# Second softmax by way of DRAM, PSUM banks of a batch end dealt out anew, last rows with W_out itself

## Chip, cores and metric

One core of a Trainium2 chip. The time is that of one execution on the device, in microseconds; lower is better.

## What is computed

x is [8, 8, 512, 64] (batch, head, token, dim), state [8, 8, 32, 64]. Per batch and head both attend to each other, and the 544 rows of a batch, heads side by side, go through one wide layer:

```python
a  = softmax(scale * x @ state.T)      # 512 x 32, scale = 1/8
xread = a @ state                      # token rows
a2 = softmax(scale * state @ x.T)      # 32 x 512, the second softmax
sread = a2 @ x                         # state rows
X = concat([xread, sread], axis=2)     # [8 * 544, 512] after heads are laid side by side
h = X @ w_in                           # 512 -> 2048
g = where(h >= 1, h, where(h <= -1, 0, (h + 1)**2 / 4))
out = g @ w_out                        # 2048 -> 512
```

All is float32. A product is made of three fast ones: both factors are split into a high and a low part, and high x high, low x high and high x low are summed.

## The kernel before

The work runs over batches b = 0 to 7 of 512 token rows, then b = 8, the 256 state rows of all batches together. Each batch has 8 steps (b, j), of 256 hidden columns each. Batch 0 is put in order by a planner with costs (`Plan`); from batch 1 on the order is that of the program: `direct` for batch 1, `sevenfold` for batches 2 to 8. Each engine runs its own instructions in program order, and a tile's buffer is handed on when its last reader is done.

A step of `sevenfold` has on TensorE: the first product (`Seven.product(0)`, 6 matmuls of 512 columns), half of the outer product of the step before (`outer(0)`), the second product, `outer(1)`. The outer product is done by seven block products instead of eight, over sums of g and of W_out's quarters; 42 matmuls of 256 columns. Their seven results stay in PSUM for the whole batch: 1 and 2 in the double buffer "mm", 7 in one of two "h" buffers, 4, 6, 5 and 3 in the four "acc" buffers, in this order (L745 to L749). `Gather` reads them out at the first step of the next batch, with three kinds of work: copies on ScalarE (`keep`, L784), additions on VectorE (`add`, L792), and four accumulating DMAs on POOL (`join`, L801); SP then writes the rows out (L806).

The sums of W_out's quarters are made in batch 1 (`fold_whole` to `fold_low`) and kept in DRAM in the tensors "fold", [128, 2, 7, 256] per chunk of 256 hidden columns; `load_wide` (L659) brings two tiles wd of 896 KB for each step, called two steps ahead, on SP.

The batch end, `stretch`, comes after the first step of a batch. TensorE reads the states of this batch (`read2`, sr, L401), multiplies the states into w_in for seven chunks and the next batch's first (`sw_product`, L449, four of them), and makes the next batch's scores (`att_start`, sc, L233), which ScalarE parks in SBUF (`park_all`, L243). Each state product is split by a cast (`sw_high`) and a subtraction (`sw_low`). sr and the "h" buffers, the first state product and the scores in "mm", the others in "acc" follow one another.

The second softmax: scores are on partitions by head pair and state; after exp, `turn_blocks` or `blocks_all` transposes 32 x 32 blocks into eb, and `shuffle` (L389) sends the blocks to the partitions of their tokens with 16 DMAs from SBUF to SBUF in runs of 128 bytes (32 KB each): batches 0 to 2 on SP, the others on POOL. For batch 0 the target is srT's buffer. `place2` (L419) sends the state rows of a batch into srT with 16 DMAs of 4 KB on POOL. SP's order in batch 1 is: shuffle of batch 0 in step 4, copies into "fold" (L636, L637), shuffle of batch 2 in step 5, "fold" again, tokens xn of batch 2 (L190) and the first wd.

The last rows (b = 8) take the same path as the others in 8 steps with 128 columns instead of 256, each w_in chunk split by `wi_split`; at the end `gather_states` makes the rows by one copy and nine additions and writes them in 16 DMAs of 32 KB.

Of the kernel before, what the change touches and what calls it, by code (L numbers as in the profile page):

```python
# [100 lines left out]
def state_exchange_moe(  # L101
# [73 lines left out]
    wo = {}  # L175

# [27 lines left out]
    class Attention:  # L204
# [10 lines left out]
        def scores(self, half=None):  # L215
            b = self.b
            if half != 1:
                sc = ps_mm(f"sc{b}")
                self.sc = [[sc[:, hh]] for hh in range(2)]
                self.z = work.tile([P, 2, S], F32, tag="z", bufs=1, name=f"z{b}")  # L220
                self.m1 = small.tile([P, 2 * NM], F32, tag="m1", name=f"m1_{b}")
                self.s1 = small.tile([P, 2 * NM], F32, tag="s1", name=f"s1_{b}")
            else:
                for hh in range(2):
                    self.sc[hh].append(ps_h(f"sc{b}_{hh}"))
            for pr in range(NPR):
                for hh in range(2):
                    rows = slice(hh * 64, hh * 64 + 64)
                    o = self.sc[hh][-1][pr * NS:(pr + 1) * NS]
                    m = self.xt[rows, :, pr]  # L230
                    if half is not None:
                        o, m = o[:, :S // 2], m[:, half]
                    nc.tensor.matmul(o, lhsT=sb[rows, b, pr], rhs=m, start=True, stop=True)  # L233
# [66 lines left out]
        def blocks_all(self):  # L300
            self.blocks = work.tile([P, 2, S], F32, tag="tmp", name=f"eb{self.b}")
            nc.vector.transpose(
                out=self.blocks.rearrange("p q t -> p (q t)"), in_=self.e2.rearrange("p q t -> p (q t)")
            )
# [69 lines left out]
        def turn_blocks(self, q):  # L374
            if q == 0:
                self.blocks = work.tile([P, 2, S], F32, tag="tmp", name=f"eb{self.b}")
            nc.vector.transpose(out=self.blocks[:, q], in_=self.e2[:, q])

        def shuffle(self):
            b = self.b  # L380
            self.r2 = small.tile([P, 2], F32, tag=own("r2", b), name=f"r2_{b}")
            nc.vector.tensor_scalar_add(self.r2, self.sum2, 1e-9)
            nc.vector.reciprocal(out=self.r2, in_=self.r2)
            src, dst = (
                v.rearrange("p q (t r n) -> p (q t) r n", r=NPR, n=NS) for v in (self.blocks, self.e2)
            )
            for r in range(NPR):
                for pr in range(NPR):
                    (nc.gpsimd if b > 2 else nc.sync).dma_start(  # L389
                        out=dst[r * NS:(r + 1) * NS, :, pr], in_=src[pr * NS:(pr + 1) * NS, :, r]  # L390
                    )

        def read2(self):
            b = self.b
            xn = loaded.pop(("xn", b))
            self.sr = ps_h(f"sr{b}")[:, :2 * D].rearrange("p (q d) -> p q d", q=2) if b else ps_mm(f"sr{b}")[:, :, :D]
            for q in range(2):
                for t in range(NT):
                    for pr in range(NPR):
                        rows = slice(pr * NS, (pr + 1) * NS)  # L400
                        nc.tensor.matmul(  # L401
                            self.sr[rows, q], lhsT=self.e2[:, q, t * P + pr * NS:t * P + (pr + 1) * NS],
                            rhs=xn[t][:, 2 * pr + q], start=t == 0 and (not b or q == 0), stop=t == NT - 1 and (not b or q == 1),
                        )
# [10 lines left out]
        def place2(self):  # L415
            b = self.b
            for k in range(P // NS):
                for pr in range(NPR):
                    nc.gpsimd.dma_start(  # L419
                        out=srT[k * NS:(k + 1) * NS, pr, b], in_=self.rt[pr * NS:(pr + 1) * NS, k * NS:(k + 1) * NS]  # L420
                    )


# [232 lines left out]
    def load_wide(b, c):  # L656
        pair = [wop.tile([P, 7, 256], F32R, tag="wo", name=f"wd{b}_{c}_{i}") for i in range(2)]
        for i in range(2):
            nc.sync.dma_start(out=pair[i].bitcast(F32), in_=folded[c][:, i])  # L659
        wide[b, c] = pair  # L660

    class Seven:
# [145 lines left out]
    def gather_states():  # L808

        o = rawp.tile([P, 2, DM], F32, tag="raw", name="o_states")  # L810
        e = work.tile([P, 3, 256], F32, tag="tmp", name="e_states")
        k = {m: v[:, :256] for m, v in banks[B].items()}

        def quad(t, d):
            return o[:, t, d * 256:(d + 1) * 256]

        def put(t, d):
            for i in range(4):
                r0 = (4 * t + i) * TOK + S
                (nc.sync if i % 2 else nc.scalar).dma_start(  # L820
                    out=out[r0:r0 + NS, d * 256:(d + 1) * 256], in_=quad(t, d)[i * NS:(i + 1) * NS]
                )

        def add(to, a, c, op=ALU.add):
            nc.vector.tensor_tensor(out=to, in0=a, in1=c, op=op)

        nc.scalar.copy(out=e[:, 0], in_=k[1])
        add(e[:, 1], k[7], e[:, 0])
        add(quad(0, 0), k[2], e[:, 0])
        put(0, 0)  # L830
        add(e[:, 2], k[4], e[:, 1])
        add(quad(1, 0), k[6], e[:, 2])
        put(1, 0)
        add(e[:, 0], k[6], e[:, 0])
        add(e[:, 1], k[6], e[:, 1])
        add(e[:, 0], k[5], e[:, 0])
        add(quad(1, 1), k[5], e[:, 1])
        put(1, 1)
        add(quad(0, 1), e[:, 0], k[3])
        put(0, 1)  # L840

    outs = {}

    def store(b, t):
        if b and t % 2 == 0:
# [131 lines left out]
    def att_start(b, half=None):  # L977
        if half != 1:
            atts[b] = Attention(b)
        atts[b].scores(half)  # L980
# [160 lines left out]
    steps = [(b, j) for b in range(1, B + 1) for j in range(NJ)]  # L1141
# [64 lines left out]
    for b in range(2, B):  # L1206
        attention(b)
    later("low", 1, 0, (fold_whole, 0))
# [24 lines left out]
    for i, s in enumerate(order[3:]):  # L1233
        later("last", *order[i + 1], (load_wide, *s))
# [4 lines left out]
    for c in range(2, NJ):  # L1239
        later("end", B, c - 2, (wi_split, c))  # L1240

    def rest(b, c):
        sw_high(b, c)
        sw_low(b, c)

    def stretch(b, between=None):
        final = b + 1 == B
# [5 lines left out]
        if not final:  # L1253
            att_start(b + 1)
        rest(b, 3)
        sw_product([(b, 7), (b + 1, 0)][:1 if final else 2], ps_acc, "raw")
        if between:
            between.high(1)
            between.low(1)
            between.last_sums()  # L1260
        atts[b].scale2()
        rest(b, 5)
        if not final and between:
            atts[b + 1].park_all()
        rest(b, 7)
# [21 lines left out]
    def sevenfold(b, j, prior, before):  # L1287
# [3 lines left out]
        first = j == 0 and b < B  # L1291
        now.product(0)
        now.curve(0)
        if old and old.b < B:
            old.high(2)
        now.bound(0)
        now.first_sum()
        if old and old.b < B:
            old.low(2)
        if b == B:  # L1300
            now.last_sums()
            for k in range(3):
                now.high(k)
                now.low(k)
            old.outer(0)
            if gather:
                gather.keep(1)
                gather.keep(7)
                gather.add(2)
            old.outer(1)  # L1310
            if gather:
                gather.add(6)
                gather.keep(4)
                gather.add(5)
                gather.keep(3)
                joins(gather, b)
            return now
# [27 lines left out]
        if first:  # L1345
            stretch(b, now)
# [5 lines left out]
        return now  # L1352

    with guard:
        plan.emit(warm)
        before = None
        for i, (b, j) in enumerate(steps):
            prior = steps[i - 1] if i else (0, NJ - 1)
            if b == 1:
                direct(b, j, prior)  # L1360
            else:
# [7 lines left out]
        before.outer(0)  # L1369
        before.outer(1)  # L1370
        gather_states()
# [43 lines left out]
```

## Time and profile before

| | us |
|---|---|
| three runs, median | 652.5 (652.27 to 653.89) |
| the profiled execution | 650.2 |
| its span | 648.4 |
| TensorE busy | 619.6 |
| VectorE busy | 517.8 |
| ScalarE busy | 475.4 |
| POOL busy | 158.4 |

Busy is the time in which an engine works on at least one instruction. PE is TensorE, PEld its weight loads, DVE VectorE, ACT ScalarE; SPq marks DMAs that SP issues. A DMA issue is not counted as busy time. Matmuls are pipelined: the length of one (283 or about 395 ns) is longer than the distance between the starts of two that follow one another.

### The profile page before, as it was taken

Reading aid. Unit: us, or ns where it says so; the run is one execution under the profiler, and the core shown is the slowest. Engines: PE = TensorE matmul, PEld = TensorE weight load, DVE = VectorE, ACT = ScalarE, POOL = GpSimd, SP = SyncE. Lnnn points to the kernel's source line nnn. Section 1 sums busy time; section 2 is a strip of 40 time slices with the busy share of each in tenths; the row PEclk is TensorE's granted clock in tenths of the full one; section 3 lists DMA queues with packets and bytes.
Section 4 is the critical chain, followed back from the end, with each engine's and each line's share of the span. In section 5 each row is a group of like instructions: output and inputs, shape, how many; then the busy total and the mean of one; then the engine's idle time right before and its main releaser. Section 6 shows DMA issues by size and latency. Waiting matters only on the chain.

```text
span 648.4 us, 13420 instructions
## 1 busy us (share of the span) xinstructions
PE 619.6 (96%) x5226; PEld 536.7 (83%) x5226; DVE 517.8 (80%) x824; ACT 475.4 (73%) x779; POOL 158.4 (24%) x260
## 2 busy tenths in 40 slices
PE   8999999998699999999999999999999999999994
PEld 3677787886579997999889997999799979999993
DVE  6999969895569977898689867987889777677773
ACT  6998766763567778787778777877877776777772
POOL 0000203111031501635162535250343206000100
PEclk9999999998999999999999999999999999999998
DMA  8993387877999887899879987999689986964985
GB/s 350 415 410 123 95 266 259 290 212 180 291 415 376 264 297 235 233 309 316 298 243 285 271 340 207 288 298 346 201 235 265 336 294 155 312 254 165 340 291 196
DMA packets 61967, 177.57 MB, mean 274 GB/s; under 512 B 22608, under 2 KB 31440, under 8 KB 58960
## 3 DMA queue, kind: packets, MB, share of 16 engines
q1 hardware_dynamic: 44576, 153.31, 67.9%
q0 software_dynamic: 16800, 23.08, 14.7%
q8 instruction: 41, 0.67, 0.4%
q10 hardware_dynamic: 528, 0.33, 0.2%
q14 instruction: 22, 0.18, 0.1%
HBM read 139.46 MB, written 26.21 MB: 256 GB/s over the span
## 4 chain that ended last, share of the span: by engine, by line
PE 76%; DVE 5%; DMA 3%; SPq 2%; ACT 2%; issue 2%; DVEq 0%; ACTq 0%
PE p L763 13%; PE p L762 13%; PE p L761 13%; PE h L692 8%; PE h L693 8%; PE h L694 8%; PE sw L449 4%; SPq L389 2%; PE acc L604 2%; PE acc L602 2%; PE acc L603 2%; DMA wd<-fold 2%; PE sr L401 1%; PE sc L233 1%; PE h L514 1%
## 5 line engine op out<-in xcount | busy, mean ns | idle before, releaser
L713 DVE SCALAR_TENSOR_TENSOR sums<-sums,over 128x512 f32<-128x512 f32 x104 | 71.7, 689 | 69.2 <-ACT sums L709 67.7
L762 PE MATMUL p<-wd,gh 128*128 128x256 f32 x416 | 117.9, 283 | 3.3 <-DMA wd<-fold 3.3
L763 PE MATMUL p<-wd,gl 128*128 128x256 f32 x416 | 117.7, 283 | 0.0
L761 PE MATMUL p<-wd,gh 128*128 128x256 f32 x416 | 117.3, 282 | 0.0
L734 ACT CAST gh<-sums 128x512 fp32r<-128x512 f32 (+1 forms) x112 | 65.6, 592 | 60.3 <-DVE sums L713 33.1
L707 ACT ACTIVATE sums<-h,half 128x512 f32<-128x512 f32 x104 | 71.8, 690 | 36.8 <-PE h L694 36.0
L763 PE MATMUL p<-wd,gc 128*128 128x256 f32 x312 | 88.8, 285 | 0.7 <-DVE gc L738 0.7
L761 PE MATMUL p<-wd,gc 128*128 128x256 f32 x312 | 88.3, 283 | 0.0
L762 PE MATMUL p<-wd,gc 128*128 128x256 f32 x312 | 88.3, 283 | 0.0
L762 PEld LDWEIGHTS p<-wd,gh 128*128 128x128 f32 x416 | 79.3, 191 | 7.4 <-DMA wd<-fold 3.7
L761 PEld LDWEIGHTS p<-wd,gh 128*128 128x128 f32 x416 | 79.3, 191 | 4.1
L763 PEld LDWEIGHTS p<-wd,gl 128*128 128x128 f32 x416 | 79.3, 191 | 0.0
L419 POOL DMA_DIRECT2D srT<-rt x128 | 63.2, 509 | 65.2 <-DVE rt L413 31.6
L738 DVE TENSOR_TENSOR gl<-sums,gh 128x512 fp32r<-128x512 f32 (+1 forms) x112 | 71.8, 647 | 0.7 <-ACT gh L734 0.7
L708 ACT ACTIVATE over<-h,less_one 128x512 f32<-128x512 f32 x104 | 70.9, 682 | 0.0
L709 ACT ACTIVATE sums<-sums 128x512 f32<-128x512 f32 x104 | 65.6, 631 | 0.0
L389 POOL DMA_DIRECT2D e<-eb x80 | 46.5, 587 | 72.2 <-ACT sums L709 51.5
L763 PEld LDWEIGHTS p<-wd,gc 128*128 128x128 f32 x312 | 59.8, 192 | 1.2 <-DVE gc L738 0.9
L761 PEld LDWEIGHTS p<-wd,gc 128*128 128x128 f32 x312 | 59.8, 192 | 0.0
L762 PEld LDWEIGHTS p<-wd,gc 128*128 128x128 f32 x312 | 59.8, 192 | 0.0
L604 PE MATMUL acc<-wo,gl 128*128 128x512 f32 x128 | 50.5, 395 | 0.5 <-DVE gl L564 0.5
L602 PE MATMUL acc<-wo,gh 128*128 128x512 f32 x128 | 50.7, 396 | 0.0
(260 smaller groups left out, 1473.8 us busy)
## 6 DMA issues: line engine op xcount, KB each, us to landing
wd<-fold SPq DMA_DIRECT2D x112, 896.0 KB, 7.8
xt<-in_xt_dram SPq DMA_DIRECT2D x16, 512.0 KB, 5.1
raw_i<-in_moe_w_in_dram SPq DMA_DIRECT2D x8, 1024.0 KB, 9.6
raw_o<-in_moe_w_out_dram SPq DMA_DIRECT2D x8, 1024.0 KB, 12.2
out_dram<-o SPq DMA_DIRECT2D x32, 256.0 KB, 4.8
fold<-wa POOLq DMA_DIRECT2D x8, 1024.0 KB, 5.9
xn<-in_x_dram SPq DMA_DIRECT2D x7, 1024.0 KB, 6.7
fold<-wo SPq DMA_DIRECT2D x8, 512.0 KB, 7.0
```

The source lines that it names most:

```text
L419: nc.gpsimd.dma_start(out=srT[k * NS:(k + 1) * NS, pr, b], in_=self.rt[pr * NS:(pr + 1) * NS, k * NS:(k + 1) * NS])
L602: nc.tensor.matmul(a, lhsT=lh, rhs=oh, start=f == 0, stop=False)
L604: nc.tensor.matmul(a, lhsT=ll, rhs=oh, start=False, stop=f == NF - 1)
L707: nc.scalar.activation(out=g, in_=h, func=AF.Relu, scale=0.5, bias=half)
L708: nc.scalar.activation(out=r, in_=h, func=AF.Relu, scale=1.0, bias=less_one)
L709: nc.scalar.activation(out=g, in_=g, func=AF.Square)
L713: nc.vector.scalar_tensor_tensor(out=g, in0=g, scalar=1.0, in1=r, op0=ALU.min, op1=ALU.add)
L734: nc.scalar.copy(out=gh, in_=s)
L738: nc.vector.tensor_tensor(out=gl, in0=s, in1=gh.bitcast(F32), op=ALU.subtract)
L761: nc.tensor.matmul(o, lhsT=gh[:, sl], rhs=wh, start=opens, stop=False)
L762: nc.tensor.matmul(o, lhsT=gh[:, sl], rhs=wl, start=False, stop=False)
L763: nc.tensor.matmul(o, lhsT=gl[:, sl], rhs=wh, start=False, stop=closes)
```

## The change

Four parts. `shuffle` writes the transposed blocks to a DRAM tensor "moved" in one DMA and reads them back in four, in runs of 1 KB; the transposition before it lays the blocks so that this works, and `read2` takes its columns accordingly. `place2` writes the rows of a batch to DRAM ("rows2") in one DMA, and `place_all` reads all batches' into srT in 16 DMAs on SP in step (7,2). At the batch end from batch 2 on, `stretch_between` takes the place of `stretch`: sr and the scores lie in "acc", the first state product in "h", the second in "mm"; state product 7 is split in step 1 of the batch ("curved"), and the third cast and subtraction (`high(2)`, `low(2)`) of step 0 come before it; banks 6 and 4 change places. `rest` casts and subtracts bank by bank. The last rows go in 4 steps (`last_rows`) of two chunks each, with plain products against W_out (`g2`), of which the missing quarter is now kept in "fold" as an eighth part, and are stored straight from two banks.

```diff
+    rows2 = drams.tile([B, P, P], F32, tag="rows2", bufs=1, name="rows2")
...
-            nc.vector.transpose(out=self.blocks[:, q], in_=self.e2[:, q])
+            nc.vector.transpose(out=self.by_rank(self.blocks, q), in_=self.as_read(q))
...
             for r in range(NPR):
-                for pr in range(NPR):
-                    (nc.gpsimd if b > 2 else nc.sync).dma_start(
-                        out=dst[r * NS:(r + 1) * NS, :, pr], in_=src[pr * NS:(pr + 1) * NS, :, r]
-                    )
+            queue = nc.gpsimd if b > 2 else nc.sync
+            moved = drams.tile([P, NPR, 2 * NT * NS], F32, tag="moved", bufs=2, name=f"moved{b}")
+            queue.dma_start(out=moved, in_=self.blocks.rearrange("p q t -> p (q t)"))
+            dst = self.e2.rearrange("p q t -> p (q t)").rearrange("p (s x) -> p s x", s=NPR)
+            src = moved.rearrange("(s n) r x -> r n s x", n=NS)
+                queue.dma_start(out=dst[r * NS:(r + 1) * NS], in_=src[r])
...
         def place2(self):
+            nc.gpsimd.dma_start(out=rows2[self.b], in_=self.rt)
+    def place_all():
+        for k in range(P // NS):
+            for pr in range(NPR):
+                nc.sync.dma_start(
+                    out=srT[k * NS:(k + 1) * NS, pr],
+                    in_=rows2[:, pr * NS:(pr + 1) * NS, k * NS:(k + 1) * NS].rearrange("b n m -> n b m"),
+                )
...
-        kept = folded[c] = drams.tile([P, 2, 7, 256], F32, tag="fold", name=f"fold{c}")
+        kept = folded[c] = drams.tile([P, 2, 8, 256], F32, tag="fold", name=f"fold{c}")
         nc.sync.dma_start(out=kept[:, :, 0:1], in_=w4[:, :, 0:1])
         nc.sync.dma_start(out=kept[:, :, 1:3], in_=w4[:, :, 2:4])
+        nc.sync.dma_start(out=kept[:, :, 7:8], in_=w4[:, :, 1:2])
...
-                for m in (4, 6, 5, 3):
+                for m in (6, 4, 5, 3):
...
+    def load_whole(c):
+        w = wo[c] = wop.tile([P, 2, 2, DM], F32R, tag="wo", name=f"wn{c}")
+        for i in range(2):
+            nc.sync.dma_start(out=w4[:, i, 0:2], in_=folded[c][:, i, 0:8:7])
+        nc.sync.dma_start(out=w4[:, :, 2:4], in_=folded[c][:, :, 1:3])
...
+    def stretch_between(b, now):
+        final = b + 1 == B
+        atts[b].read2(ps_acc)
+        atts[b].scale2()
+        sw_product([(b, 1), (b, 2)], ps_h)
+        rest(b, 1)
+        if not final:
+            att_start(b + 1, apart=ps_acc)
+            atts[b + 1].park_all()
+        now.last_sums()
+        sw_product([(b, 3), (b, 4)])
+        rest(b, 3)
+        now.high(1)
+        now.low(1)
+        now.high(2)
+        sw_product([(b, 5), (b, 6)], ps_acc, "xn")
+        rest(b, 5)
+        now.low(2)
+        sw_product([(b, 7), (b + 1, 0)][:1 if final else 2], ps_acc, "raw")
...
+        later("curved", b, 1, (lambda b=b: rest(b, 7),))
+    later("end", B - 1, 2, (place_all,))
...
+    def last_rows(b, j, prior, old):
+        hid = Hidden(b, j)
+        for i in range(2):
+            hid.product(i)
+            hid.relu(i)
+            hid.square(i)
+            hid.bound(i)
...
+            if old:
+                old.outer(i)
...
+        hid.high()
+        hid.low()
+        if not old:
+            issue("mid", b, j)
+            g2(*prior)
```

## Rows read from the trace of the kernel before

**Rows 1.** Waits of all engines: engine, line, waited for, us in total, times, longest.

```profile
ACT sums L707 <- PE h L694: 36.0, 83, 1.5
...
PE p L762 <- DMA wd<-fold: 3.3, 2, 1.7
...
PE p L763 <- DVE gc L738: 0.7, 1, 0.7
```

**Rows 2.** Windows: stretch, its length, busy us, granted clock, DMA share, GB/s.

```profile
16.00:33.00 17.00, 15.82 (x88) 10.33 (x86) 16.75 (x24) 16.94 (x25) 0.00 (x0) 1.00 1.01 415
...
148.00:152.00 4.00, 4.00 (x19) 3.34 (x18) 0.41 (x1) 0.90 (x1) 0.00 (x0) 1.00 1.01 254
...
156.00:160.00 4.00, 4.00 (x65) 3.08 (x66) 3.81 (x5) 1.92 (x4) 0.00 (x0) 0.57 0.38 72
...
326.00:388.00 62.00, 62.00 (x430) 57.88 (x431) 52.98 (x83) 48.53 (x83) 28.82 (x51) 1.00 0.94 297
```

**Rows 3.** Timeline of TensorE, ends of batches 1 and 2: start, length, idle before.

```profile
152.51 0.39 PE L516 MATMUL h<-atl,sw_7hl 128*128 128x512 f32 x1
155.32 1.94 PE L401 MATMUL sr<-xn,srT 128*32 128x64 f32 x64 [2.43 <-DMA srT<-eb]
...
160.21 0.40 PE L603 MATMUL acc<-wo,gh 128*128 128x512 f32 x1
...
172.03 0.39 PE L604 MATMUL acc<-wo,gl 128*128 128x512 f32 x1
177.81 2.14 PE L401 MATMUL sr<-xn,e 128*32 128x64 f32 x64 [5.39 <-ACT o L850]
...
186.31 0.50 PE L692 MATMUL h<-ath,sw_1h 128*128 128x512 f32 x1
```

**Rows 4.** Timeline of SP's DMA issues, batch 1.

```profile
135.98 16.17 SPq L389 DMA_DIRECT2D srT<-eb  x16
...
153.73 13.37 SPq L389 DMA_DIRECT2D e<-eb  x16
...
168.51 1.34 SPq L190 DMA_DIRECT2D xn<-in_x_dram  x1
```

**Rows 5.** Timeline of VectorE, batch 1.

```profile
156.19 0.71 DVE L340 STREAM_TRANSPOSE zt<-z 128x512 f32<-128x512 f32 x1 [7.78 <-DMA fold<-wo]
```

**Rows 6.** Timeline of all engines, 163 to 190 us: the last of ACT's copies.

```profile
175.71 1.09 ACT L850 COPY o<-acc 128x512 f32<-128x512 f32 x2
```

**Rows 7.** Timeline of TensorE, the end of batch 4.

```profile
318.94 1.10 PE L401 MATMUL sr<-xn,e 128*32 128x64 f32 x64
...
323.67 1.09 PE L233 MATMUL sc<-xt,sb 64*32 64x512 f32 x16 [0.88 <-PE sw L449]
...
325.84 0.50 PE L692 MATMUL h<-ath,sw_1h 128*128 128x512 f32 x1
```

**Rows 8.** Timeline of TensorE, the end of batch 7.

```profile
527.59 1.10 PE L401 MATMUL sr<-xn,e 128*32 128x64 f32 x64
...
532.87 1.26 PE L449 MATMUL sw<-w,sb 64*32 64x256 f32 x16 [1.43 <-DVE sw_3l L476]
```

**Rows 9.** DMA issues: tile, queue, count, KB each, median us from issue to landing.

```profile
wd<-fold SPq DMA_DIRECT2D x112, 896.0 KB, 7.8
...
flat<-wf POOLq DMA_DIRECT2D x5, 512.0 KB, 3.0
wa<-flat POOLq DMA_DIRECT2D x5, 512.0 KB, 7.5
```

**Rows 10.** Timeline of all engines, 638 us to the end.

```profile
639.63 0.28 PE L763 MATMUL p<-wd,gl 128*128 128x256 f32 x1
...
641.78 0.28 PE L763 MATMUL p<-wd,gc 128*128 128x256 f32 x1
641.85 3.90 SPq L820 DMA_DIRECT2D out_dram<-o_states  x8
```

**Rows 11.** Waits of SP's queue.

```profile
SPq L806 <- DMA o<-spare: 17.2, 6, 10.6
```

More of the change, by code (lines that the diff above doesn't have):

```diff
@@ L213, in __init__, with scores @@
             att_of[b] = (self.ath, self.atl)
-        def scores(self, half=None):
+        def scores(self, half=None, apart=None):
             b = self.b
             if half != 1:
-                sc = ps_mm(f"sc{b}")
-                self.sc = [[sc[:, hh]] for hh in range(2)]
+                sc = None if apart else ps_mm(f"sc{b}")
+                self.sc = [[apart(f"sc{b}_{hh}") if apart else sc[:, hh]] for hh in range(2)]
                 self.z = work.tile([P, 2, S], F32, tag="z", bufs=1, name=f"z{b}")
@@ L301, in blocks_all, with by_rank, as_read @@
             self.blocks = work.tile([P, 2, S], F32, tag="tmp", name=f"eb{self.b}")
-            nc.vector.transpose(
-                out=self.blocks.rearrange("p q t -> p (q t)"), in_=self.e2.rearrange("p q t -> p (q t)")
-            )
+            nc.vector.transpose(out=self.by_rank(self.blocks), in_=self.as_read())
+        def by_rank(self, v, q=None):
+            v = v.rearrange("p q t -> p (q t)").rearrange("p (r x n) -> p x r n", r=NPR, n=NS)
+            return v if q is None else v[:, q * NT:(q + 1) * NT]
+        def as_read(self, q=None):
+            v = self.e2.rearrange("p q t -> p (q t)").rearrange("p (x r n) -> p x r n", r=NPR, n=NS)
+            return v if q is None else v[:, q * NT:(q + 1) * NT]
         def top1(self, q, half=None):
@@ L658, in load_wide @@
         for i in range(2):
[L659 removed]
+            nc.sync.dma_start(out=pair[i].bitcast(F32), in_=folded[c][:, i, 0:7])
         wide[b, c] = pair
+    def load_whole(c):
+        w = wo[c] = wop.tile([P, 2, 2, DM], F32R, tag="wo", name=f"wn{c}")
+        w4 = w.bitcast(F32).rearrange("p i a (h c) -> p i (a h) c", h=2)
+        for i in range(2):
+            nc.sync.dma_start(out=w4[:, i, 0:2], in_=folded[c][:, i, 0:8:7])
+        nc.sync.dma_start(out=w4[:, :, 2:4], in_=folded[c][:, :, 1:3])
     class Seven:
@@ L806, in write, with store @@
                 nc.sync.dma_start(out=out[r0:r0 + P, :], in_=self.o[:, t])
[L808 to L817, printed above, removed]
+    outs = {}
+    def store(b, t):
+        if b == B:
+            if t == 0:
+                outs[b] = rawp.tile([P, 2, DM], F32, tag="raw", name=f"o{b}")
+            o = outs[b][:, t]
+            nc.scalar.copy(out=o, in_=acc[b][t])
             for i in range(4):
                 r0 = (4 * t + i) * TOK + S
[L820 to L844, printed above, removed]
+                (nc.sync if i % 2 else nc.scalar).dma_start(out=out[r0:r0 + NS, :], in_=o[i * NS:(i + 1) * NS])
+            return
         if b and t % 2 == 0:
@@ L975, in state_exchange_moe, with att_start @@
     atts = {}
-    def att_start(b, half=None):
+    def att_start(b, half=None, apart=None):
         if half != 1:
             atts[b] = Attention(b)
-        atts[b].scores(half)
+        atts[b].scores(half, apart)
     def att_ops1(b):
@@ L1137, in state_exchange_moe @@
     read(("eb", 1), 2.0, lambda: atts[1].shuffle(), after=[("blocks", 1, 0), ("blocks", 1, 1)])
-    steps = [(b, j) for b in range(1, B + 1) for j in range(NJ)]
+    steps = [(b, j) for b in range(1, B + 1) for j in range(NJ if b < B else NJ // 2)]
     background = {}
@@ L1233, in state_exchange_moe @@
     for i, s in enumerate(order[3:]):
-        later("last", *order[i + 1], (load_wide, *s))
+        if s[0] < B:
+            later("last", *order[i + 1], (load_wide, *s))
+        else:
+            later("last", *order[i + 1], (load_whole, 2 * s[1]), (load_whole, 2 * s[1] + 1))
+    later("end", B - 1, 2, (place_all,))
     later("end", B - 1, 5, (states_split, 0))
@@ L1238, in state_exchange_moe, with stretch @@
     later("mid", B - 1, 7, (wi_split, 1))
-    for c in range(2, NJ):
-        later("end", B, c - 2, (wi_split, c))
+    for j in range(NJ // 2 - 1):
+        later("half", B, j, (wi_split, 2 * j + 2))
+        later("mid", B, j, (wi_split, 2 * j + 3))
     def rest(b, c):
[L1243 to L1247, printed above, removed]
+        for pt, wh, wl in sw_of[b, c]:
+            nc.scalar.copy(out=wh, in_=pt)
+            nc.vector.tensor_tensor(out=wl, in0=pt, in1=wh.bitcast(F32), op=ALU.subtract)
+    def stretch(b):
         atts[b].read2()
@@ L1252, in stretch @@
         rest(b, 1)
-        if not final:
-            att_start(b + 1)
+        att_start(b + 1)
         rest(b, 3)
[L1256 to L1260, printed above, removed]
+        sw_product([(b, 7), (b + 1, 0)], ps_acc, "raw")
         atts[b].scale2()
         rest(b, 5)
-        if not final and between:
-            atts[b + 1].park_all()
-        rest(b, 7)
+        rest(b, 7)
+    def stretch_between(b, now):
[6 more added lines that the diff above has]
+            att_start(b + 1, apart=ps_acc)
+            atts[b + 1].park_all()
+        now.last_sums()
[8 more added lines that the diff above has]
+        sw_product([(b, 7), (b + 1, 0)][:1 if final else 2], ps_acc, "raw")
     def direct(b, j, prior):
@@ L1291, in sevenfold @@
         first = j == 0 and b < B
+        late = old and old.b < B and old.j > 0
         now.product(0)
         now.curve(0)
-        if old and old.b < B:
+        if late:
             old.high(2)
         now.bound(0)
+        issue("curved", b, j)
         now.first_sum()
-        if old and old.b < B:
+        if late:
             old.low(2)
[L1300 to L1317, printed above, removed]
         issue("f0", b, j)
@@ L1345, in sevenfold @@
         if first:
-            stretch(b, now)
+            stretch_between(b, now)
         else:
@@ L1352, in sevenfold @@
         return now
+    def last_rows(b, j, prior, old):
+        hid = Hidden(b, j)
+        gather = Gather(prior[0]) if old else None
+        for i in range(2):
+            hid.product(i)
+            hid.relu(i)
+            hid.square(i)
+            if old and i == 0:
+                old.high(2)
+            hid.bound(i)
+            if old and i == 0:
+                old.low(2)
+            if i == 0:
+                issue("half", b, j)
+            if old:
+                old.outer(i)
+                for f, m in ((gather.keep, 1), (gather.keep, 7), (gather.add, 2)) if i == 0 else ((gather.add, 6), (gather.keep, 4), (gather.add, 5), (gather.keep, 3)):
+                    f(m)
+        if old:
+            issue("mid", b, j)
+            joins(gather, b)
+        hid.high()
+        hid.low()
+        if not old:
+            issue("mid", b, j)
+            g2(*prior)
     with guard:
@@ L1360, in state_exchange_moe @@
                 direct(b, j, prior)
+            elif b == B:
+                last_rows(b, j, prior, before)
+                before = None
             else:
@@ L1368, in state_exchange_moe @@
             issue("last", b, j)
-        before.outer(0)
-        before.outer(1)
-        gather_states()
+        g2(*steps[-1])
 _INS = ["x", "xt", "state", "moe_w_in", "moe_w_out"]
```

17 lines of the change are left out of this document (4 added, 13 removed).

## The prediction

> **What bounds the kernel now.** I read the windows first. From 326 to 388 us, a batch in mid-course, TensorE is busy for 62.00 of 62.00 us at full clock [rows 2]: there the kernel is TensorE's own work, and nothing that another engine saves shows in the time. What can be saved lies in the few holes, so I looked for those next, in TensorE's timeline. It holds three kinds.
>
> First, around the end of batch 1. The last product of step (1,7) starts at 152.51; the state read of batch 0 (sr, 64 matmuls) comes only at 155.32, after 2.43 us of waiting for the DMAs srT<-eb [rows 3]. Behind this hole the granted clock falls: the window 156 to 160 has 0.57, close to the lower of the two levels, 1.2 of 2.4 GHz [rows 2]. Then from 172.03 to 177.81 the state read of batch 2 waits 5.39 us, by the view for ACT's copies o<-acc [rows 3], which end at 176.80 [rows 6].
>
> Both have one root, to be seen on SP's queue. The second softmax of batch 0 reaches its partitions in 16 DMAs, issued over 16.17 us from 135.98; that of batch 2 takes 16 more, 13.37 us from 153.73; the tokens of batch 2 (xn) are queued behind them and leave only at 168.51 [rows 4]. As long as the first 16 run, they hold one of two "tmp" buffers, and VectorE waits 7.78 us for it before 156.19 [rows 5]. That delay goes on through ACT to the copies at 175.71 [rows 6].
>
> Second, every batch end: scores wait 0.88 us for the only "mm" buffer [rows 7]; in batch 7 the last state product waits 1.43 us [rows 8].
>
> Third, the last rows: 3.3 us for wd<-fold, 0.7 for gc [rows 1], and after the last matmul (641.78) a chain of additions whose last store leaves SP at 641.85 + 3.90 = 645.75 [rows 10].
>
> **The change, part by part.** Lengths used: a 512-column matmul takes (172.03 - 160.21) / 52 = 0.227 us, a 256-column one (641.78 - 639.63) / 18 = 0.119 us (52 and 18 are the matmuls between the rows named) [rows 3, 10].
>
> *Shuffle through DRAM, batches 0 and 2.* Sixteen issues become five: a write of 512 KB, a wait for its landing on the same queue, four reads of 128 KB. No row has this round trip. Below, its write has the 3.0 us of flat<-wf (512 KB out); above, 7.5, the length of wa<-flat (512 KB in) [rows 9]; the reads likewise. An issue costs 13.37 / 16 = 0.84 to 16.17 / 16 = 1.01 us [rows 4]. From 135.98 batch 0's blocks are in place by 135.98 + 3.0 + 3.4 + 3.0 = 145.4 at best, by 135.98 + 7.5 + 4.0 + 7.5 = 155.0 at worst; needed at 152.51 + 0.23 = 152.74. I take a value near the lower end, since the nearest row for the write is flat<-wf, same size and direction. Queued behind the wait: two (now three) copies into "fold", batch 2's shuffle and xn. With five issues each, xn leaves by about 155 instead of 168.5, and "tmp" comes free with the write's landing, so VectorE's 7.78 us go too.
> Then sr of batch 0 follows at once: 152.74 + 1.10 (its length in batch 4 [rows 7]) + 7 x 0.227 = 155.43 stands where 160.21 stands now, the slow clock included: **-4.8 us**.
> Batch 2's end runs from 172.03 + 0.23 = 172.26 to 186.31, 14.05 us [rows 3]; in batch 4 the same work takes 325.84 - 318.94 = 6.90, and 6.02 without its wait [rows 7]. What is late next: ACT's copies end 4.5 us after TensorE's last matmul now (176.80 against 172.26); VectorE gains 7.8 and TensorE 4.8, so some 1.5 us of lateness are left. The new order needs only the first copied bank for sr, and the copies of the others by the scores, 2 us later: covered. **-8.0 us.**
> From batch 3 on the shuffle is POOL's: the wait for the write's landing holds up four reads and, behind them, only the joins of the next batch end, and sr comes three steps later. place2 falls from 16 DMAs to one. No gain, no loss.
>
> *Batch ends.* Scores get two "acc" banks, the first state product the two "h" banks, so the 0.88 us in batches 4, 5 and 6 go; batch 3 I put at 0.5, its wait being shorter; batch 7 loses its 1.43. **-2.6, -0.5, -1.4 us.** Batch 1's end stays as it is. What pays: the casts of state product 7 move into step 1, behind the first curve, and the third cast and subtraction of step 0 come ahead of it. ACT waited 36.0 us in 83 places for a product, 0.43 each [rows 1]; TensorE now arrives 0.9 earlier, so ACT's lead is used up at step 1, and the "h" bank may be late for the next product. Bound: nothing to 1 us a batch; I take 0.2, six times: **+1.2 us**.
>
> *Last rows.* The products stay (192 of 256 columns). The outer ones go from 8 x 21 x 0.119 = 20.0 us to 4 x 24 x 0.227 = 21.8: **+1.8**. The loads fall from 14.7 to 8.4 MB and no longer sit behind the writes of batch 7, which SP held for up to 10.6 us until the joins landed [rows 11]; the waits of 3.3 and 0.7 go: **-4.0**. Step 1 may wait for its second split weight (bound 0 to 2 us, taken as none: the split is due 0.3 us late at worst by the order of ACT's work).
> The tail: last matmul's end to last issue now is 645.75 - 642.06 = 3.7; then one copy (1.09 / 2 = 0.55 [rows 6]), 0.2 of waits, two issues at 3.90 / 8 = 0.49 a queue [rows 10]: 1.7. The difference is 2.0; the stores being twice as long, I take **-1.8**.
>
> *Costed at nothing.* The third copy into "fold" (8 issues of SP, 2 MB) lies where 22 of 32 issues vanish. Transpositions with permuted blocks: no row has one; if they doubled, VectorE would lose 2 x 0.71 us a batch [rows 5], beside gap-free TensorE. place_all puts 16 issues on SP in step 2 of batch 7, 13 to 16 us at the rates above; SP reaches them a step early, so the next load leaves 8 us late at most, and it has two steps' lead (15.7 us) less 7.8 of landing [rows 9]. It just fits; without that cover, up to 7 us.
> *The pitch of "fold".* A partition's row grows from 14 to 16 KB, a power of two, and 7 KB of it are read 96 times in batches 2 to 7. TensorE takes 896 KB x 2 = 1.835 MB per step of ((527.59 - 318.94) / 3 - 6.90) / 8 = 7.83 us [rows 7, 8], 234 GB/s. The first weights, rows of 8 KB, also a power of two, come at 415 GB/s with the engines full (16 to 33 us) [rows 2]. I cost it at nothing. The Trainium skill (DMA: Bandwidth & Descriptors, Latency and other measured facts) speaks against it: copies between DRAM tensors fall to 207 GB/s at a row pitch of 512 KiB and lower at larger powers of two. By that figure, as an estimate, a pair would take 8.9 us and 48 steps lose 51 us; the trace's 415 GB/s is against it at 8 KB, and no row shows 16 KB.
>
> Sum: -4.8 - 8.0 - 2.6 - 0.5 - 1.4 + 1.2 + 1.8 - 4.0 - 1.8 = **-20.1 us**. The profiled execution took 650.2 us (span 648.4), so 630.1; the median of the runs, 652.5, is 2.3 above it, so about 632.4. I say 632.
>
> **Rivals.**
> (a) The round trip is late. At the upper end, batch 0's blocks land at 155.0, 2.3 us late, and the slow clock comes back with it: the 4.8 are lost; batch 2's xn, queued behind two such trips, costs another 2. For it: the engines are full there now (148 to 152: share 1.01 at 254 GB/s [rows 2]). Against: it is the short runs that fill them so. 632 + 6.8, about 639.
> (b) Batch ends are not shortened, only moved: ACT and VectorE fall behind at step 1 by 1 us a batch and the batch-end gain (4.5) goes. For: VectorE and ACT have much to do there. Against: ACT's 36.0 us of waiting for TensorE. 632 + 4.5 - 1.2 + 6 x 0.4, about 638.
> (c) Slower: the loads from the 16 KB rows fall below what TensorE takes. The point from which it decides the sign: 20.1 / 48 = 0.42 us more per step, 8.25 us a pair, under 222 GB/s. For: the loads are two thirds of a batch's traffic, and the engines are 0.94 busy with it at 297 GB/s [rows 2]. Just past the point the time is 655; at half of those 297, 12.4 us a pair, 632 + 48 x 4.6 = 853. Against: the 415 GB/s at 8 KB. [...]
> (d) The holes move but don't close: something other than the shuffle keeps batch 2 back (xn, or loads of wd), 632 + 8 = 640, and with (b) 646.
>
> **Chances.** Forecast 0.64; (a) 0.13; (b) 0.12; (c) 0.05; (d) 0.06. A measurement of this kernel tells 0.3%, 2 us. All but (c) are faster, and a heap of (a), (b), (d) together could come near no change: faster 0.92, within 0.3% 0.03, slower 0.05. Range: below, no new waits and a further 3 us where ACT and VectorE run on unhindered, 626; above, (a) with half of (b), 643.
>
> **What would show it.** Right: sr of batch 0 directly behind the product, no window near 0.57; sr of batch 2 without a wait; batch ends of 6.0 to 6.2 us between sr and the next product; no wait for wd<-fold; a tail under 2 us between last matmul and last issue. Wrong: a wait of sr for the DMA e<-moved; ACT-bound gaps of TensorE before the product of step 2; waits for wd<-fold in every step (c) or in steps 4 and 5 of batch 7 (place_all).

## Result and profile after

The changed kernel takes **630.9 us** (median of four runs, 629.59 to 632.28) where the one before, on the same chip, takes 653.2 (652.27 to 654.63): a ratio of 0.966 with a 95% interval of 0.963 to 0.969. The prediction said 632, range 626 to 643. The profiled execution took 631.4 us with a span of 629.5; before it was 650.2 and 648.4, so 18.9 us of span are gone against the 20.1 of the sum. Between the medians it is 22.3: the 650.2 of the profile lies below all four timed runs of the kernel before, so the two traces leave out 3.4 us. In two later series the mean granted clock of the kernel before was 0.983 to 0.994 (0.992 in the profile), in the one that timed the changed kernel again its clock was 0.996 to 1.000; part of the 3.4 us may lie there, which is not shown.

The page, totals by engine and the clock in 40 slices:

```profile
PE 614.4 (98%) x5154; PEld 531.8 (84%) x5154; DVE 499.3 (79%) x765; ACT 464.4 (74%) x746; POOL 66.4 (11%) x85
...
PEclk9999999999999999999999999999999999999999
```

TensorE's busy time fell by only 5.2 us (619.6 before): 13.7 of the 18.9 us that went are idle time. The clock is at 0.9 or more in every slice and 1.000 in the mean. Windows of the whole core (us, then each engine's busy time, the granted clock, DMA share, GB/s), to be set beside [rows 2]:

```profile
148.00:152.00 4.00, 4.00 (x20) 3.30 (x19) 4.00 (x6) 2.49 (x4) 0.00 (x0) 1.00 1.05 412
152.00:156.00 4.00, 4.00 (x78) 3.14 (x77) 3.87 (x7) 3.94 (x6) 0.67 (x1) 1.00 1.01 403
156.00:160.00 4.00, 4.00 (x19) 3.34 (x18) 3.47 (x6) 0.43 (x1) 0.64 (x1) 1.00 0.95 293
```

The hole is closed and its slow clock (0.57 at 156 to 160) with it. The DMA engines are as full as they were (148 to 152), but now move 412 GB/s instead of 254. It was not the old shuffle's short runs that filled them. The view of the DMA queues of the kernel before in 148 to 152 us (packets, MB, share of the engines' time) has

```profile
q0 software_dynamic: 258, 0.99, 96.1%
q1 hardware_dynamic: 238, 0.03, 4.9%
```

SP issues nothing but the shuffle there, and its queue, q1, takes 4.9%; the rest is q0, POOL's, on which a write of 1 MB into "fold" is under way (145.63 to 152.19). TensorE's timeline, ends of batches 1 to 4, and the first step of batch 7:

```profile
152.66 0.39 PE L524 MATMUL h<-atl,sw_7hl 128*128 128x512 f32 x1
152.98 1.10 PE L408 MATMUL sr<-xn,srT 128*32 128x64 f32 x64
...
167.51 0.39 PE L612 MATMUL acc<-wo,gl 128*128 128x512 f32 x1
170.12 1.10 PE L408 MATMUL sr<-xn,e 128*32 128x64 f32 x64 [2.22 <-issue]
...
176.46 1.50 PE L457 MATMUL sw<-w,sb 64*32 64x256 f32 x41 [1.66 <-issue]
177.89 0.50 PE L708 MATMUL h<-ath,sw_1h 128*128 128x512 f32 x1
...
245.65 1.91 PE L457 MATMUL sw<-w,sb 64*32 64x256 f32 x50 [0.58 <-issue]
247.49 0.50 PE L708 MATMUL h<-ath,sw_1h 128*128 128x512 f32 x1
...
310.39 1.10 PE L408 MATMUL sr<-xn,e 128*32 128x64 f32 x64
311.42 1.09 PE L457 MATMUL sw<-w,sb 64*32 64x256 f32 x32
...
313.17 2.80 PE L457 MATMUL sw<-w,sb 64*32 64x256 f32 x96
315.89 0.50 PE L708 MATMUL h<-ath,sw_1h 128*128 128x512 f32 x1
...
521.39 0.39 PE L777 MATMUL p<-wd,gh 128*128 128x256 f32 x1 [0.50 <-DVE sw_3l L1242]
```

sr of batch 0 follows its product without a wait; sr of batch 2 still waits 2.22 us, and a wait of 1.66 follows within that batch end. Batch 4's end, sr to next product, takes 5.50 us instead of 6.90. The same landmarks in both traces say where the time went:

| stretch, to the start of | before | after | gain in it | predicted |
|---|---|---|---|---|
| the last product of batch 1 | 172.03 | 167.51 | 4.5 | 4.8 |
| step (2,1) | 186.31 | 177.89 | 3.9 | 8.0 |
| step (3,1) | 256.16 | 247.49 | 0.25 | 0.5 - 0.2 |
| step (6,1) | 464.91 | 452.31 | 3.9 | 3 x (0.88 - 0.2) |
| step (7,1) | 534.06 | 519.24 | 2.2 | 1.4 - 0.2 |
| the end of the span | 648.4 | 629.5 | 4.1 | 4.0 |

(The 0.2 is a sixth of the 1.2 us of small waits. The sixth share, batch 7's, falls into the last row and is not taken off there.) One stretch is far off: batch 2's end. SP's queue there, issue start and length, against [rows 4]:

```profile
136.06 0.33 SPq L393 DMA_DIRECT2D moved<-eb  x1
138.74 2.98 SPq L397 DMA_DIRECT2D srT<-moved  x4
...
144.08 1.51 SPq L393 DMA_DIRECT2D moved<-eb  x1
155.17 2.74 SPq L397 DMA_DIRECT2D e<-moved  x4
...
159.86 1.11 SPq L191 DMA_DIRECT2D xn<-in_x_dram  x1
```

Batch 0's write is in DRAM 2.7 us after its issue; batch 2's takes 11.1, with the queue standing behind it. xn leaves at 159.86, not at "about 155". The view of xn's load gives its landings:

```profile
DMA to landing us min/median/max: 4.8/6.1/10.2
```

159.86 + 10.2, the longest, is 170.06, and sr starts at 170.12; the longest is that of batch 2's own load. In the kernel before it took 9.1: 168.51 + 9.1 = 177.6, and sr started at 177.81 [rows 3]. So it may have been xn there too, and not the copies of ScalarE that the row names; no run tried that in the kernel before. Last, DMA issues (KB each, median us to landing) and the tail:

```profile
wd<-fold SPq DMA_DIRECT2D x96, 896.0 KB, 8.0
...
moved<-eb SPq DMA_DIRECT2D x3, 512.0 KB, 3.9
...
srT<-moved SPq DMA_DIRECT2D x4, 128.0 KB, 7.6
```

```profile
624.75 0.39 PE L612 MATMUL acc<-wn,gl 128*128 128x512 f32 x1
625.17 0.58 ACT L831 COPY o<-acc 128x512 f32<-128x512 f32 x1 [2.13 <-PE acc L612]
625.78 0.78 SPq L834 DMA_DIRECT2D out_dram<-o  x2
625.79 0.85 ACTq L834 DMA_DIRECT2D out_dram<-o  x2
```

wd lands in 8.0 us against 7.8 [rows 9], TensorE waits for it nowhere, and the last issue ends 1.5 us after the last matmul (624.75 + 0.39 to 626.64).

### The profile page after: what moved, and what is told of

It reads as the page before. It is cut to its first block, busy times and chain, and to the rows that moved or that the text cites. A ratio compares the mean times of both kernels' runs of the same rounds, so it can differ in the third digit from the quotient of the medians.

```text
span 629.5 us, 12904 instructions
## 1 busy us (share of the span) xinstructions
PE 614.4 (98%) x5154; PEld 531.8 (84%) x5154; DVE 499.3 (79%) x765; ACT 464.4 (74%) x746; POOL 66.4 (11%) x85
## 4 chain that ended last, share of the span: by engine, by line
PE 75%; DVE 5%; DMA 4%; issue 2%; ACT 2%; SPq 1%; DVEq 0%; ACTq 0%
PE p L777 13%; PE p L779 13%; PE p L778 13%; PE h L708 7%; PE h L709 7%; PE h L710 7%; PE sw L457 4%; PE acc L612 2%; PE acc L610 2%; PE acc L611 2%; DMA moved<-eb 2%; PE h L523 2%; PE h L522 2%; PE h L524 2%; DMA fold<-wo 1%
## 5 line engine op out<-in xcount | busy, mean ns | idle before, releaser
L777 PE MATMUL p<-wd,gh 128*128 128x256 f32 x384 | 108.5, 283 | 0.5 <-DVE sw_3l L1242 0.5
L778 PE MATMUL p<-wd,gh 128*128 128x256 f32 x384 | 108.7, 283 | 0.0
L779 PE MATMUL p<-wd,gl 128*128 128x256 f32 x384 | 108.6, 283 | 0.0
L750 ACT CAST gh<-sums 128x512 fp32r<-128x512 f32 x96 | 59.9, 624 | 57.6 <-DVE sums L729 33.3
L779 PE MATMUL p<-wd,gc 128*128 128x256 f32 x288 | 81.6, 283 | 0.0
L777 PE MATMUL p<-wd,gc 128*128 128x256 f32 x288 | 81.6, 283 | 0.0
L778 PE MATMUL p<-wd,gc 128*128 128x256 f32 x288 | 81.5, 283 | 0.0
L777 PEld LDWEIGHTS p<-wd,gh 128*128 128x128 f32 x384 | 72.9, 190 | 4.7 <-DVE sw_3l L1242 0.9
L778 PEld LDWEIGHTS p<-wd,gh 128*128 128x128 f32 x384 | 72.9, 190 | 3.8
L779 PEld LDWEIGHTS p<-wd,gl 128*128 128x128 f32 x384 | 72.9, 190 | 0.0
L754 DVE TENSOR_TENSOR gl<-sums,gh 128x512 fp32r<-128x512 f32 x96 | 65.8, 685 | 4.8 <-ACT gh L750 4.8
L777 PEld LDWEIGHTS p<-wd,gc 128*128 128x128 f32 x288 | 54.9, 191 | 0.0
L779 PEld LDWEIGHTS p<-wd,gc 128*128 128x128 f32 x288 | 54.9, 190 | 0.0
L778 PEld LDWEIGHTS p<-wd,gc 128*128 128x128 f32 x288 | 54.9, 191 | 0.0
L539 ACT ACTIVATE u<-h,half 128x512 f32<-128x512 f32 x40 | 27.0, 686 | 33.4 <-PE h L524 22.8
L610 PE MATMUL acc<-wo,gh 128*128 128x512 f32 x128 | 50.2, 392 | 0.0
L611 PE MATMUL acc<-wo,gh 128*128 128x512 f32 x128 | 49.9, 390 | 0.0
```

The source lines that it names most:

```text
L610: nc.tensor.matmul(a, lhsT=lh, rhs=oh, start=f == 0, stop=False)
L611: nc.tensor.matmul(a, lhsT=lh, rhs=ol, start=False, stop=False)
L750: nc.scalar.copy(out=gh, in_=s)
L754: nc.vector.tensor_tensor(out=gl, in0=s, in1=gh.bitcast(F32), op=ALU.subtract)
L777: nc.tensor.matmul(o, lhsT=gh[:, sl], rhs=wh, start=opens, stop=False)
L778: nc.tensor.matmul(o, lhsT=gh[:, sl], rhs=wl, start=False, stop=False)
```

## Experiments

**Each part alone.** Three kernels take one part of the change into the kernel before; all were timed in one series, where the kernel before took 653.6. The profiled execution of each is the longest of its four, and that of the kernel before lies below its median, so a span set beside 648.4 shows less gain than the medians do. The theories are in spans.

The shuffle through DRAM, with `place_all`:

```diff
-                for pr in range(NPR):
-                    (nc.gpsimd if b > 2 else nc.sync).dma_start(
-                        out=dst[r * NS:(r + 1) * NS, :, pr], in_=src[pr * NS:(pr + 1) * NS, :, r]
-                    )
+            queue.dma_start(out=moved, in_=self.blocks.rearrange("p q t -> p (q t)"))
...
+                queue.dma_start(out=dst[r * NS:(r + 1) * NS], in_=src[r])
```

> The kernel before with the DRAM shuffle, rows2 and place_all alone; batch ends and last rows as before. Theory (SP's queue made both early holes): the state read of batch 0 follows its product without a wait (4.6 us back), the state read of batch 2 waits 1 to 2.5 instead of 5.4 us, the later batch ends stay at 6.9 us, the last rows keep their 3.3 us of waiting for wd: span about 640 (648.4 before). Rival (batch 2's end needs the new banks as well): only the first 4.6 come back, span 643.5 to 644.

640.8 us, ratio 0.981 (0.977 to 0.984), span 640.7. TensorE:

```profile
152.15 0.39 PE L524 MATMUL h<-atl,sw_7hl 128*128 128x512 f32 x1
152.47 1.04 PE L408 MATMUL sr<-xn,srT 128*32 128x64 f32 x60
...
167.01 0.39 PE L612 MATMUL acc<-wo,gl 128*128 128x512 f32 x1
167.32 1.10 PE L408 MATMUL sr<-xn,e 128*32 128x64 f32 x64
```

Both holes are gone, also the 1 to 2.5 us that the theory left to sr of batch 2: this part alone does for batch 2 what the whole change doesn't. Here xn leaves SP at 155.93. "fold" gets two copies per chunk and not three, and the write of the second shuffle lands in 8.8 us (142.60 to 151.44).

The batch ends alone, with the new order of banks and casts:

```diff
-            stretch(b, now)
+            stretch_between(b, now)
```

> The kernel before with the new batch ends alone (stretch_between, banks in the order 6, 4, 5, 3, state product 7 split in step 1). Theory: batches 4 to 6 gain 1.25 us each, 3 gains 0.3, 7 gains 2.2, batch 2 gains its 0.9 but keeps the wait of 5 us for the tokens: span about 641.5. Rival (ends gain only with POOL and the DMA engines relieved by the other part): 0.9 a batch at most and new waits in step 2, span 644.5 to 646.

645.9 us, ratio 0.988 (0.984 to 0.992); the profiled execution, with a span of 645.6, was the longest of its four. The waits of batches 4 to 6 are gone, and batch 4's end, against 6.90, is

```profile
318.29 1.10 PE L401 MATMUL sr<-xn,e 128*32 128x64 f32 x64
...
323.85 0.50 PE L692 MATMUL h<-ath,sw_1h 128*128 128x512 f32 x1
```

5.56 us: 1.34 saved where the wait was 0.88. The rest is in the state products behind that wait. In the timeline of the kernel before, the last 32 start at

```profile
324.52 1.39 PE L449 MATMUL sw<-w,sb 64*32 64x256 f32 x32
```

and end with the product at 325.84 [rows 7], 1.32 us; in the changed kernel 96 in a row take 315.89 - 313.17 = 2.72, or 0.91 per 32. No wait at step 1 came of it but 0.50 in batch 7. The span is 4.1 us above the expected one. In this trace other waits grew: sr of batch 2 by 0.5, wd in the last rows by 0.6, and two of 0.41 and 0.29 for gl. Behind the first two the clock was also low for longer: 0.50 in 176 to 180 us and 0.75 in 180 to 184 (0.63 and 0.94 in the kernel before, behind the same hole), and 0.91 in 600 to 640 (1.00 before). Between the medians the gain is 7.6 us, about the 6.9 of the theory.

The last rows alone, `last_rows` and `g2` with the eighth part of "fold" that they read:

```diff
+        nc.sync.dma_start(out=kept[:, :, 7:8], in_=w4[:, :, 1:2])
```

> The kernel before with the last rows alone, fold with its eighth part and 16 KB rows. Theory: the waits for wd go, outer products cost 1.8 us more, the tail is some 2 us shorter: 4.1 us less, span about 644.3; batch 1 and the batch ends as before. Rival (rows of 16 KB slow the loads): wd lands 1 us later or more than the 7.8 of before and TensorE waits for wd in batches 2 to 7, span above 648.

647.4 us, ratio 0.991 (0.988 to 0.994), span 646.4. The span is some 2 us above the theory's; between the medians the gain is 6.2 us, more than the theory's 4.1, so whether it fell short isn't settled. The waits for wd and gc are gone, and no load of wd is waited for in any batch. What costs time in this trace is far from the last rows. sr of batch 2 waits 9.1 us instead of 5.39:

```profile
179.29 1.00 PE L401 MATMUL sr<-xn,e 128*32 128x64 f32 x23 [9.11 <-issue]
```

with SP's queue ahead of it

```profile
152.41 13.59 SPq L389 DMA_DIRECT2D e<-eb  x16
166.04 0.63 SPq L636 DMA_DIRECT2D fold<-wo  x1
166.72 1.40 SPq L637 DMA_DIRECT2D fold<-wo  x1
168.16 1.37 SPq L638 DMA_DIRECT2D fold<-wo  x1
169.63 1.31 SPq L190 DMA_DIRECT2D xn<-in_x_dram  x1
```

The copy costed at nothing doesn't look free in batch 1: with it xn leaves 1.1 us later than in [rows 4], and sr of batch 2 starts 1.5 us later than in [rows 3]. The three parts alone gain 12.8, 7.6 and 6.2 us, 26.6 in sum; together 22.3. Why the sum is larger wasn't looked into.

**What holds up sr of batch 2?** Only xn's queue was changed:

```diff
-        nc.sync.dma_start(out=xn, in_=x[b])
+        (nc.gpsimd if b == 2 else nc.sync).dma_start(out=xn, in_=x[b])
```

> The changed kernel with the tokens of batch 2 (1 MB) issued on POOL's queue instead of SP's, so that they don't stand behind the shuffle of batch 2. Theory (the tokens' landing releases the state read of batch 2, not ACT's copies): they leave by 150 us instead of 159.9, the state read waits 0 to 0.6 us instead of 2.22, span 627.3 to 628. Rival (ACT's last copy releases it, as the view of before said): it still starts 1.0 us after that copy ends, wait 2.2, span 629.5.

628.1 us, one run. On POOL's queue xn leaves at 153.72, not by 150, and TensorE's timeline is

```profile
167.82 1.10 PE L408 MATMUL sr<-xn,e 128*32 128x64 f32 x64
...
173.70 1.50 PE L457 MATMUL sw<-w,sb 64*32 64x256 f32 x41 [1.20 <-issue]
175.13 0.50 PE L708 MATMUL h<-ath,sw_1h 128*128 128x512 f32 x1
...
178.01 0.39 PE L778 MATMUL p<-wd,gh 128*128 128x256 f32 x1 [1.11 <-DMA wd<-fold]
```

The 2.22 us are gone. ScalarE was not touched: its last copies stand in this trace as in that of the changed kernel,

```profile
167.99 1.09 ACT L841 COPY o<-acc 128x512 f32<-128x512 f32 x2
```

and sr now starts before they end. So it was xn. A new wait of 1.11 for wd gives part of it back. In a later series of five rounds:

> The kernel after with batch 2's xn on POOL's queue, timed: 2.7 us less than the kernel after on the same chip (2.22 ahead of sr and some of the 1.66 behind it, against a new wait of 1.11 for wd), ratio about 0.962. Were the look at it chance, it would stand within 1 us of the kernel after.

628.0 us (628.00 to 628.87), ratio 0.9635 (0.962 to 0.965), and on the same chip

> The kernel after itself, on the chip of the two kernels above, so that the three ratios can be set side by side: 0.966, about 630.9.

630.6 us (629.09 to 631.59), ratio 0.967 (0.965 to 0.969). The two sets of runs don't overlap: this one line is worth 2.6 us and beats both kernels. In this second profile of the changed kernel sr of batch 2 waited 2.58 us, and xn again landed just ahead of it (170.73):

```profile
170.82 1.93 PE L408 MATMUL sr<-xn,e 128*32 128x64 f32 x64 [2.58 <-issue]
```

Behind the wait the granted clock fell, to 0.82 in 168 to 172 us and 0.75 in 172 to 176, and sr took 1.93 us where it took 1.10 in the first profile. So the wait costs more than its length in some executions.

**Issues or bytes?** Is the third copy in the way by its issue or by its transfer? The parts of "fold" were laid in another order, so that two of the copies are one DMA of the same bytes:

```diff
-        nc.sync.dma_start(out=kept[:, :, 0:1], in_=w4[:, :, 0:1])
-        nc.sync.dma_start(out=kept[:, :, 7:8], in_=w4[:, :, 1:2])
+        nc.sync.dma_start(out=kept[:, :, 6:8], in_=w4[:, :, 0:2])
```

> The kernel after with the third copy into fold folded into the first (the parts lie so that the two are one DMA): the same bytes, 8 issues of SP fewer, two of them ahead of batch 2's xn. If the third copy keeps xn back by its issue time, xn leaves SP some 1.5 us earlier (by 158.4 instead of 159.86) and the wait of 2.22 us ahead of sr of batch 2 shrinks to about 0.7; time 1.5 us less, about 629. If it does so by its bytes (they lie ahead of the shuffle's write, 11.08 us to land), xn leaves at most 0.7 us earlier and the wait stays above 1.4; about 630.5.

631.9 us, one run, no gain. SP's queue:

```profile
143.11 0.82 SPq L393 DMA_DIRECT2D moved<-eb  x1
154.89 3.27 SPq L397 DMA_DIRECT2D e<-moved  x4
...
159.59 0.80 SPq L191 DMA_DIRECT2D xn<-in_x_dram  x1
```

The write leaves 1 us earlier and lands at about the same time as before, 154.89 against 155.17 (153.83 in the second profile of the changed kernel); xn leaves 0.27 earlier, and the wait is 2.90 us. So two issues fewer didn't help; that the bytes are what counts was not tried by itself. Both changes together:

> The kernel after with batch 2's xn on POOL's queue and the merged copy: sr of batch 2 without a wait for xn, as with xn on POOL's queue alone; the wd load that came 1.11 us late there leaves SP 1.4 us earlier. If issue time was what made it late the wait goes and the time is about 627; if the transfer itself (18 us in a full stretch) it stays near 1 us and the time is that of the next kernel, about 628.

630.4 us (629.30 to 631.53), ratio 0.967 (0.965 to 0.970): the gain of xn's queue is lost again, as now the shuffle's own reads come last:

```profile
169.81 0.38 PE L408 MATMUL sr<-xn,e 128*32 128x64 f32 x13 [1.90 <-DMA e<-moved]
```

The write's landing is 155.14 here and 153.24 with xn on POOL's queue alone. Both of my alternatives missed this: with the engines full (share 1.05 in 144 to 154 us), one load's gain came with another's delay. Why a write that is issued 1 us earlier lands up to 2 us later isn't settled; the landings of the same write in the two profiles of the changed kernel are 1.3 us apart already. That copies of 512 KB now lie ahead of it where some were of 256 KB would be one reason, and it wasn't tried.

**The split of state product 7.** Put back at the batch end, out of step 1:

```diff
-        later("curved", b, 1, (lambda b=b: rest(b, 7),))
+        rest(b, 7)
```

> The changed kernel with the split of state product 7 back at the batch end, ahead of step 1's first curve on ACT and VectorE. Theory (TensorE now comes early, so ACT has no lead left there): two casts of 1.07 us together delay the curve, and TensorE waits 0.3 to 1 us for the bank of the next product in each of six batches, span 631.5 to 635.5. Rival (ACT has slack enough): no new waits, span 629 to 630.

631.25 us, one run, span 629.5, as the changed kernel's, with no new wait, and the 0.50 us in batch 7 still there. My theory fell: ScalarE and VectorE have room at either place, and the move brings nothing by itself.

**The waits that the profile calls "issue".** Those within the batch ends (1.66 in batch 2, 0.58 in batch 3) have no producer that is late. DMA in 173 to 178 us shows a queue of its own for instructions:

```profile
q8 instruction: 1, 0.02, 1.2%
```

In the whole span it moves 41 such blocks of 16 KB, 0.67 MB. Spread over TensorE's 10308 matmuls and weight loads that is 65 bytes each; VectorE, the next, has 765 instructions, so I take the queue for TensorE's. In the trace they begin at 174.0 and 243.4, and the waits end at 176.46 and 245.65, 2.5 and 2.2 us later. To move where a block falls, the program was shifted by 84 matmuls at its start. The warm-up calls this twice, so that 96 matmuls of 64 columns stand in place of twelve of 512:

```diff
+        if n == 6:
+            for c in range(48):
+                nc.tensor.matmul(over[:, :64], lhsT=ident, rhs=ident[:, :64], start=True, stop=True)
+            return
```

> The changed kernel with six warm-up matmuls of 512 columns given as 48 of 64 columns, some 170 TensorE instructions more early in batch 0, in about the same time. Theory (the waits of 1.66 us in batch 2's end and 0.58 in batch 3's, which no release explains, are TensorE waiting for its own instructions, fetched in blocks of 16 KB): the blocks begin at other places, so one of the two waits at least goes or changes by over 0.4 us, and one may turn up in another batch end. Rival (a buffer or an engine releases them): both stay within 0.1 us. Time within 1.5 us of the changed kernel either way.

653.5 us, one run. The expected time was missed. The 96 narrow matmuls take 20.74 us at full clock, 0.216 each, where the twelve took 5.42, and the end of batch 1 comes 16 us later:

```profile
7.05 20.74 PE L164 MATMUL warmed<-ident 128*128 128x64 f32 x96
```

What was asked, though, is where the waits are:

```profile
332.97 0.67 PE L461 MATMUL sw<-w,sb 64*32 64x256 f32 x16 [1.18 <-issue]
...
402.49 1.08 PE L461 MATMUL sw<-w,sb 64*32 64x256 f32 x26 [1.21 <-issue]
```

Now batches 3 to 6 wait 2.08, 1.18, 1.21 and 1.71 us in the middle of their state products, where the changed kernel waited 0.58 in batch 3 and not at all in 4 to 6; batch 2's state products no longer wait, and its next product waits 0.45. Their blocks begin at 259.5, 330.6, 400.1 and 470.4, and the waits end at 261.99, 332.97, 402.49 and 472.81: 2.4 to 2.5 us after, each time. Nothing that these batch ends compute or load was changed, so a late producer of data is out. That TensorE waits there for its own instructions is the reading that fits all six; the trace has no event that says so. That the shift moved them rests on batches 4 to 6: without it, none of seven profiles with the new batch ends and last rows has such a wait there. In batches 2 and 3 the waits also differ between executions of one program: in the second profile of the changed kernel batch 2's state products don't wait and batch 3's wait 0.90.

## Why the prediction came out as it did

- **sr of batch 0** (4.8 predicted, 4.5 measured). Right, the clock too. The write landed in 2.7 us, just below the range that I took (3.0 to 7.5); the reads took 7.6 (median), just above it. With 138.74 + 2.98 + 7.6 = 149.3 us they were still there before 152.74, so the first half of rival (a) fell. What was said against that rival, that the short runs fill the engines, was misread: in 148 to 152 us they took 4.9% of the engines' time. VectorE's wait of 7.78 us is gone, as said: in the changed kernel that transposition starts at 148.47 without a wait. [rows 5] names the copy into "fold" there, which stood behind the same sixteen issues.
- **Batch 2's end** (8.0 predicted, 3.9 measured) is the term that failed, and of it the sentence on what is late next. I let ScalarE's copies decide, as the row named them, and took xn's leave at "about 155" as settled. It left at 159.86 and released sr itself. Two assumptions failed: that the second write lands like the first (3.0 us taken, 7.5 the upper end; 11.1 in fact), and, as it seems, that the third copy into "fold" is free: without it, in the shuffle alone, xn leaves 3.9 us earlier and the wait is gone, but no run took out that copy by itself. That xn ends the wait is shown: with xn on POOL's queue, behind the same write and the same three copies, it goes. There the stretch from the last matmul (167.73) to the next product (175.13) is 7.4 us, or 6.2 without the instruction wait, against the 14.05 - 8.0 = 6.05 of the prediction. Rival (d) named xn and was given 0.06; it was half true. So was the second half of rival (a), that xn is queued behind a late round trip. The 1.66 us within this batch end were in no term.
- **Batch ends 3 to 7** (4.5 less 1.2 for small waits predicted, 6.4 measured). The waits went as said. The forecast was too small: the state products behind the wait had run slower too, 0.41 per 32, which I did not look for in the rows; and the small waits at step 1 did not come but for 0.50 in batch 7. Rival (b) fell: with the split of product 7 at either place nothing changed.
- **Last rows and tail** (4.0 predicted, 4.1 measured). Right in the sum; the tail is 1.5 us against the 1.7 worked out. No wait for wd after `place_all`.
- **The pitch of 16 KB** costs nothing: 8.0 against 7.8 us for a pair's half. Rival (c) falls with it: TensorE waits for wd in no step. The rule of the Trainium skill (DMA: Bandwidth & Descriptors, Latency and other measured facts) was carried further than it goes: beside its 207 GB/s at 512 KiB it gives 214 as the full rate of such copies, reached with a padded pitch. As an estimate from these two figures that is a loss of some 3% at 512 KiB, and of 16 KB it says nothing. Copies at its pitches were run by no kernel here.
- **The total** of the spans came out 1.2 us from the sum because the excess of 4.1 in batch 2's end was nearly met by batch ends that gave 3.1 more than forecast. That is luck, and so is the rest of the closeness: the 2.3 us added to the profiled time for the median did not come, as the median of the changed kernel, 630.9, lies 0.5 below its profiled 631.4. The holes, the batch ends and the tail were understood, one size of them wrong by half because what releases sr of batch 2 was wrong.

## What to carry to other kernels

Sixteen small DMAs in a row held SP's queue for 16.17 and 13.37 us, and all that stood behind them waited. A detour through DRAM in five issues was worth its round trip here; whether the fewer issues or the longer runs did it was not tried apart. Its cost depends on the load of the DMA engines (2.7 us for the first write at a share of 0.5, 8.8 to 12.0 for the second at 1.03 to 1.07), and everything behind its wait leaves with it. Before a full DMA is put down to one transfer, look at the shares of the queues. When a transfer is moved, add the landing time to the issue of each load that the next stage needs, and compare the sum with the stage's start; the releaser that the profile names for a wait on several things may be another one. A load that must not wait goes to a queue with no such wait ahead of it: here that was worth 2.6 us, and nothing any more when the copies ahead of it were laid otherwise.

## What was not expected of the hardware

TensorE seems to wait for its own program in stretches of short matmuls. The batch ends issue 64 state reads in 1.03 us (310.39 to 311.42 in batch 4) and 96 state products in 2.72, each matmul with a weight load; where a 16 KB instruction block begins late in such a stretch, some 2.6 to 5.2 us after sr in batches 3 to 6, TensorE stands for 0.6 to 2.1 us and goes on 2.2 to 2.5 us after the block's start. A block that begins early costs nothing: in batches 4 and 5 of the changed kernel one begins at 310.9 and 379.0, 0.4 to 0.6 us after sr, and no wait follows. In the steps, with a matmul each 0.12 to 0.23 us, blocks are read without a wait. Where a block falls changes with the program (84 matmuls more at its start) and, less, from execution to execution.
